# An mLSTM layer with a feed-forward block on one core: the output gates' load and sigmoid moved within the front, gate steps moved to GpSimd, split output weights from the ninth column block on

## The chip, the cores and the metric

The kernel runs on one core of a Trainium2 chip. The time is the device time of one execution in microseconds (us). The kernel before took 531.28 us (median of three runs, 530.12 to 533.42). The clock of TensorE that the chip grants differs between stretches of the run, and the profile shows it beside each.

## The reference

An mLSTM with 4 sequences, 8 heads of width 40 and 768 steps, and behind it a feed-forward block on the 3072 tokens:

```python
m_new = np.maximum(f_gate[:, :, t] + m, i_gate[:, :, t])
f_stab = np.exp(f_gate[:, :, t] + m - m_new)
i_stab = np.exp(i_gate[:, :, t] - m_new)
C = f_stab * C + i_stab * np.einsum('bhd,bhe->bhde', vt, kt)
n = f_stab * n + i_stab * kt
y[:, :, t] = sigmoid(o_gate) * (C @ qt) / np.maximum(np.abs(n . qt), 1.0)
...
h = x @ w_in                                  # x: 3072 x 320, w_in: 320 x 2048
g = np.where(h >= 1, h, np.where(h <= -1, 0.0, (h + 1) ** 2 / 4.0))
out = g @ w_out                               # 2048 x 320
```

The two weights arrive as float64, everything else as float32.

## The kernel before, in words

**Chunks.** The time axis is cut into 6 chunks of 128 steps. An item n = 0 to 23 is one chunk of one sequence (n // 4 is the chunk, n % 4 the sequence). Per item the kernel forms a decay matrix of 128 x 128 for each head (`Abc`: the running sum `ac` of the log decays, written to DRAM as `a_d` and read back broadcast over the partitions, masked by a select on GpSimd, and exponentiated on ScalarE with a bias `nA`), the scores q k (`score`), and in `main` the three parts of the output: `ip`, the carried state times q (`psa<-C,qn`); `up`, values times decayed scores (`psa<-v,Abc`); then on VectorE `hv`, the denominator `z`, `sz`, `y`; then the transpose `psa<-ident,y` and the copies `xh`, `xl` of the result in two words, which the feed-forward block multiplies. `carry_on` makes the new state (`psa<-v,vk`, then `C`). All these products go through the two PSUM buffers `psa`, in turn.

**Gates.** Per chunk, `gate_sums`, `gate_tail` and `gate_exps` (lines 186 to 246) work on 32 x 128 tiles: a scan for m, a clamp and rounding to a grid (`ah`), a scan for `ac`, the rest `a` (stored in `fi_t`) and its scan `al` (stored in `ah`), and the exponents `ex`, which TensorE transposes and ScalarE exponentiates into `G`, the scales of k, v and of the outputs. `dc` is the chunk's total decay; ScalarE makes `dx`, its exponential, which goes through DRAM into `dec`, the factor of the state. In the kernel before all steps but three copies run on VectorE, two of the copies on ScalarE for chunks 1 to 5.

**The feed-forward block.** It runs in six stages j = 0 to 5 of 512 tokens (four items each: stage j multiplies the outputs of items 4j to 4j+3), each with 16 column blocks fc of 128 hidden units. `mm1` (lines 660 to 672) makes eight 128x512 products into one of two `psh` buffers; ScalarE makes relu and its square, VectorE the last step of `r`, which frees the buffer. `mm2` follows two blocks later into four `pso` accumulators. Products are made in two fast words: x is `xh` + `xl`, w_in `wh` + `wl`, w_out `oh` + `ol` and r `gh` + `gl` (`parts`, lines 674 to 679), which gives three passes `oh,gh`, `ol,gh` (named `ow` in the profile) and `oh,gl`. For the first PLAIN_FC blocks of stage 0, r and w_out are multiplied as plain float32 instead, without `gh`, `gl` and without the split of w_out, which is done in stage 1 (lines 801 to 804).

**The weights.** Each of the 16 pieces (8 of w_in for two blocks each, 8 of w_out) is loaded raw (`wraw`, two buffers, two pieces ahead) and turned into float32 words by `words`: `mg` on ScalarE, sign bits (`win<-wraw`, `ow<-wraw`) on VectorE, low bits on GpSimd, then two steps on VectorE; `split` then makes the two fast words, a copy on ScalarE and a subtraction on VectorE. `split_next` (lines 704 to 712) issues one piece; the loop at line 794 calls it until DUE(fc) pieces have been issued. The order of use is in0, in1, out0, in2, out1 and so on.

**What sets the order.** The front (everything before stage 0) is a list of steps by hand, `STEPS`, issued in exactly that order on each engine: L.. are loads, E, A, x the decays of chunk 0, s and m the scores, g and k the gates, o the sigmoid of chunk 0, c and e and d a piece of weights, u, y, z, t the four parts of `main`. Behind it the loop at lines 790 to 821 emits the feed-forward block, and `slot` puts the steps of the items of later chunks between its blocks by the table OFFS. The framework's scheduler then fixes each engine's order by its own estimate of times; `behind` and `issue_after` hold an instruction back behind a named one of the same engine.

Of the kernel before, what the change touches and what calls it, by code (L numbers as in the profile page):

```python
# [13 lines left out]
ALU = mybir.AluOpType  # L14
# [5 lines left out]
L = 128  # L20
# [10 lines left out]
CLAMP = -128.0  # L31

LAG = 2

PLAIN_FC = 16

# [9 lines left out]
ST = 0  # L46

GFC = 3
DUE = lambda fc: 3 + fc

STEPS = (
# [3 lines left out]
)  # L58

HALF = 64  # L60
# [3 lines left out]
GRID = 49152.0  # L64
# [31 lines left out]
def mlstm_ffn_kernel(ctx, tc, qk, qn, vk, og, fi0, fi, w_in, w_out, cst, out):  # L96
# [82 lines left out]
    gtail = {}  # L179

    def gate_piece(c):
        gate_sums(c)
        gate_tail(c)
        gate_exps(c)

    def gate_sums(c):
        pool, i, f = gsrc.pop(c)

        NP = NSEQ if c else 3 * NSEQ
        new = lambda name, p=NP, n=L, bufs=1: pool.tile([p, n], F32, name=name if c else name + "0", bufs=bufs)  # L190
        k = 1
        m, a, ah, ac = new("m", n=L + 1, bufs=k), f, new("ah", bufs=k), new("ac")
        al = ah

        ex = exs[c] = new("ex", P)
        if c:
            nc.vector.tensor_copy(m[:, 0:1], carry)
        else:
            nc.vector.memset(m[:, 0:1], -1e30)
        nc.vector.tensor_tensor_scan(out=m[:, 1:], data0=f, data1=i, initial=m[:, 0:1], op0=ALU.add, op1=ALU.max)  # L200
        nc.vector.tensor_tensor(out=a, in0=f, in1=m[:, :L], op=ALU.add)
        nc.vector.tensor_tensor(out=a, in0=a, in1=m[:, 1:], op=ALU.subtract)

        nc.vector.tensor_scalar(out=ah, in0=a, scalar1=CLAMP, scalar2=GRID, op0=ALU.max, op1=ALU.add)
        nc.vector.tensor_scalar(out=ah, in0=ah, scalar1=-GRID, scalar2=None, op0=ALU.add)
        nc.vector.tensor_tensor_scan(out=ac, data0=rst[:NP], data1=ah, initial=0.0, op0=ALU.mult, op1=ALU.add)
        if c > 0:
            nc.sync.dma_start(a_d[c], ac)
            nc.scalar.copy(ex[64:96], ac)
        else:  # L210

            for p in (2 * NSEQ, NSEQ):
                nc.vector.tensor_tensor(out=ac[:p], in0=ac[:p], in1=top(ac[:p]), op=ALU.subtract)
            T["ac"] = ac
            m, a, ah, ac, al, i = (x[2 * NSEQ:] for x in (m, a, ah, ac, al, i))
            nc.gpsimd.tensor_copy(ex[64:96], ac)
        nc.vector.scalar_tensor_tensor(out=a, in0=a, scalar=CLAMP, in1=ah, op0=ALU.max, op1=ALU.subtract)
        reset = rst[:NSEQ] if c else rst[2 * NSEQ:]
        nc.vector.tensor_tensor_scan(out=al, data0=reset, data1=a, initial=0.0, op0=ALU.mult, op1=ALU.add)
        if c:  # L220
            nc.scalar.mul(ex[96:128], al, -1.0)
        else:
            nc.gpsimd.tensor_scalar(out=ex[96:128], in0=al, scalar1=-1.0, scalar2=None, op0=ALU.mult)
        nc.vector.tensor_copy(carry, m[:, L:])
        gtail[c] = i, m, a, ac, al, ex

    def gate_tail(c):
        i, m, a, ac, al, ex = gtail.pop(c)
        dh = m[:, :L]
        eng = nc.vector  # L230
        eng.tensor_tensor(out=a, in0=i, in1=m[:, 1:], op=ALU.subtract)
        eng.tensor_tensor(out=a, in0=a, in1=al, op=ALU.subtract)
        nc.gpsimd.tensor_copy(ex[0:32], a)
        eng.tensor_tensor(out=dh, in0=ac[:, L - 1:].broadcast_to([NSEQ, L]), in1=ac, op=ALU.subtract)
        eng.tensor_tensor(out=dh, in0=dh, in1=a, op=ALU.add)
        eng.tensor_tensor(out=ex[32:64], in0=dh, in1=al[:, L - 1:].broadcast_to([NSEQ, L]), op=ALU.add)
        eng.tensor_tensor(out=dc[:, c:c + 1], in0=ac[:, L - 1:], in1=al[:, L - 1:], op=ALU.add)
# [466 lines left out]
    def split_next(m="x"):  # L704
        nonlocal nw
        if nw < len(W_ORDER):
            with behind((m, "act"), (m, "dve")):
                for _ in convert(*W_ORDER[nw]):
                    pass
            if nw + 2 < len(W_ORDER):  # L710
                load_w(*W_ORDER[nw + 2])
            nw += 1
# [5 lines left out]
    for what in STEPS.split():  # L718
# [20 lines left out]
        elif what[0] == "m":  # L739
            score_mul(n, hh)  # L740
        elif what[0] == "g":
            gate_sums(n)
        elif what[0] == "k":
            gate_tail(n)
        elif what[0] == "h":
# [44 lines left out]
    for x in range(NG + LAG):  # L790
        j, fc = divmod(x, NFC)
        if x < NG:
            if j == 0:
                while nw < min(len(W_ORDER), DUE(fc)):
                    split_next()
                if nw == len(W_ORDER) and late is None:
                    stages.close()
                    late = ctx.enter_context(tc.tile_pool(name="late", bufs=1, side="right"))
# [9 lines left out]
                    gate_piece(j + 2)  # L808
            r = mm1(j, fc)
            if x == 0:  # L810
                with tc.issue_after(mark["r", "dve"].ins):
                    gate_tail(1)
                    gate_exps(1)
            with behind(("v", "pool")):
                slot(FRONT + x)
            gs[x] = parts(r) if j or fc >= PLAIN_FC else (r,)
# [61 lines left out]
```

## Time and profile before

| What | us |
|---|---|
| median of three runs | 531.28 |
| lowest and highest run | 530.12, 533.42 |
| the profiled execution | 535.73 |
| its span, first to last instruction | 533.9 |
| first matmul of stage 0, of stage 1 | 35.62, 151.07 |
| TensorE (PE) busy in the span | 497.4 |
| VectorE (DVE), ScalarE (ACT), GpSimd (POOL) busy | 366.4, 290.8, 146.4 |
| mean granted clock of TensorE | 0.968 |

A row of a timeline gives start, duration, engine, line, operation and out<-in by the kernel's names; in brackets the idle time before it and what ended it. Most instructions bear line 79, the line of the helper that issues them, or line 82, its branch for the hand-made order of the front; so a row is known by its names. A row of groups gives busy us, the mean of one in ns, and the idle time before.

### The profile page before, as it was taken

How to read it: one execution, taken by the hardware profiler on the slowest of the kernel's cores; microseconds unless marked ns; L12 is line 12 of the kernel's file. 1: busy time of each engine (PE TensorE's matmuls, PEld its weight loads, DVE VectorE, ACT ScalarE, POOL GpSimd, SP SyncE). 2: the span in 40 equal slices, each digit the busy share in tenths (PEclk: the TensorE clock that was granted, in tenths of full speed). 3: DMA queues.
4: the chain of work that ended last, by engine and by line, in shares of the span. 5: the costliest groups of instructions: out<-in, count | busy, mean ns of one | idle time of the engine just before them, and what ended most of it. 6: DMA issues, size and time to landing. Idle time of an engine off the chain costs nothing.

```text
span 533.9 us, 9184 instructions
## 1 busy us (share of the span) xinstructions
PE 497.4 (93%) x3527; PEld 421.8 (79%) x3527; DVE 366.4 (69%) x677; ACT 290.8 (54%) x576; POOL 146.4 (27%) x148
## 2 busy tenths in 40 slices
PE   7985989989899999989999979799999999999996
PEld 4753766768679889879888958598898898989886
DVE  4589988489759777769576848777757756444342
ACT  4525766544458664567644435754468344445553
POOL 2316522234333134343052515152411212000000
PEclk8987999979899999999999979999999999999999
DMA  7858555264342223252122234022333100010001
GB/s 218 243 162 264 182 150 170 83 207 153 85 154 68 48 61 104 79 155 76 30 78 72 84 103 152 3 83 100 111 106 114 40 0 1 2 49 2 1 1 50
DMA packets 29648, 51.31 MB, mean 96 GB/s; under 512 B 10124, under 2 KB 20004, under 8 KB 29604
## 3 DMA queue, kind: packets, MB, share of 16 engines
q1 hardware_dynamic: 29604, 50.72, 31.4%
q8 instruction: 28, 0.46, 0.3%
q14 instruction: 16, 0.13, 0.1%
HBM read 46.67 MB, written 4.04 MB: 95 GB/s over the span
## 4 chain that ended last, share of the span: by engine, by line
PE 69%; DVE 12%; ACT 8%; DMA 6%; issue 2%; POOL 1%; SPq 1%; ACTq 0%; DVEq 0%; POOLq 0%
PE psh L79 29%; PE pso L79 26%; PE psa L79 12%; ACT Abc L79 3%; DMA Abc<-a_d 2%; ACT r L79 2%; DMA wraw<-in_w_out 2%; PE pso L82 1%; DVE win L79 1%; DMA raw<-in_qk 1%; DVE r L79 1%; PE psa L82 1%; DVE mg L79 1%; POOL Abc L79 1%; DVE ow L79 1%
## 5 line engine op out<-in xcount | busy, mean ns | idle before, releaser
L79 ACT ACTIVATE r<-psh,half 128x512 f32<-128x512 f32 x96 | 65.3, 685 | 102.4 <-PE psh L79 101.1
L79 PE MATMUL psh<-xh,wh 128*128 128x512 f32 x288 | 105.6, 422 | 13.4 <-DVE r L79 12.0
L79 DVE SCALAR_TENSOR_TENSOR r<-psh,r 128x512 f32<-128x512 f32 x96 | 66.0, 687 | 65.2 <-ACT r L79 64.9
L79 PE MATMUL psh<-xh,wl 128*128 128x512 f32 x288 | 100.4, 404 | 0.0
L79 PE MATMUL pso<-oh,gh 128*128 128x320 f32 x320 | 99.4, 313 | 0.6 <-ACT gh L79 0.6
L79 PE MATMUL pso<-ow,gh 128*128 128x320 f32 x320 | 98.6, 310 | 0.0
L79 PE MATMUL pso<-oh,gl 128*128 128x320 f32 x320 | 91.1, 310 | 0.0
L79 DVE TENSOR_TENSOR gl<-r,gh 128x512 fp32r<-128x512 f32 x80 | 61.0, 765 | 28.3 <-ACT gh L79 27.7
L79 ACT CAST gh<-r 128x512 fp32r<-128x512 f32 x80 | 49.5, 618 | 51.2 <-DVE r L79 49.9
L79 PEld LDWEIGHTS psh<-xh,wh 128*128 128x128 f32 x288 | 51.8, 195 | 24.1 <-DVE r L79 14.5
L79 PEld LDWEIGHTS psh<-xh,wl 128*128 128x128 f32 x288 | 55.8, 195 | 13.1 <-DVE m L82 0.4
L79 ACT ACTIVATE Abc<-Abc,nA 128x128 f32<-128x128 f32 x160 | 49.6, 390 | 29.7 <-POOL Abc L79 29.7
L79 PEld LDWEIGHTS pso<-oh,gh 128*128 128x128 f32 x320 | 60.1, 188 | 4.5 <-ACT gh L79 0.8
L79 PE MATMUL psh<-xl,wh 128*128 128x512 f32 x192 | 62.5, 408 | 0.0
L79 PEld LDWEIGHTS pso<-ow,gh 128*128 128x128 f32 x320 | 60.1, 188 | 2.8
L79 ACT ACTIVATE r<-r 128x512 f32<-128x512 f32 x96 | 60.3, 632 | 2.2
L79 PEld LDWEIGHTS pso<-oh,gl 128*128 128x128 f32 x320 | 58.0, 188 | 0.3
L79 POOL TENSOR_TENSOR v<-vk,G 128x328 f32<-128x328 f32 x36 | 31.5, 879 | 53.6 <-issue 29.8
L79 POOL TENSOR_TENSOR m<-m 128x1024 bf16<-128x1024 f32 x16 | 31.2, 1953 | 51.8 <-DVE m L79 40.6
L79 PEld LDWEIGHTS psh<-xl,wh 128*128 128x128 f32 x192 | 37.0, 195 | 8.5
L79 PE MATMUL pso<-ow,r 128*128 128x320 f32 x128 | 39.9, 457 | 0.5 <-DVE ow L79 0.5
L79 POOL TENSOR_TENSOR C<-C,dec 120x369 f32<-120x369 f32 x16 | 13.8, 859 | 91.7 <-PE psa L79 91.7
(187 smaller groups left out, 742.0 us busy)
## 6 DMA issues: line engine op xcount, KB each, us to landing
Abc<-a_d SPq DMA_DIRECT2D x20, 512.0 KB
raw<-in_qk SPq DMA_DIRECT2D x48, 160.0 KB
vk<-in_vk SPq DMA_DIRECT2D x20, 324.0 KB
wraw<-in_w_in SPq DMA_DIRECT2D x8, 768.0 KB
wraw<-in_w_out SPq DMA_DIRECT2D x8, 640.0 KB
sig<-in_og SPq DMA_DIRECT2D x6, 640.0 KB
out<-r SPq DMA_DIRECT2D x24, 160.0 KB
qn<-in_qn SPq DMA_DIRECT2D x20, 180.0 KB
```

What stands on the lines that cost most here:

```text
L79: r = getattr(self.engine, name)(*args, **kwargs)
L82: r = getattr(self.engine, name)(*args, **kwargs)
```

## The change

It has these parts.

1. PLAIN_FC is 8 instead of 16: blocks 8 to 15 of stage 0 use the three fast passes, and the second four pieces of w_out are split in stage 0 rather than in stage 1.
2. DUE is 2 + fc instead of 3 + fc, and a piece is held behind the last step of the newest r rather than behind the newest copies of x.
3. In STEPS the load of chunk 0's output gates stands behind the loads of q and k of items 0 and 1, and its sigmoid behind the scores of item 1 instead of ahead of the first decays. The first three parts of chunk 1's gates (ga, gb, gc: `gate_sums` became a generator) and `gate_tail` (k1) are spread over the front; the step d, the subtraction wl of the first piece, comes earlier.
4. For chunks 1 to 5 all gate steps other than scans go to GpSimd, also the two copies into `ex` that ScalarE made; the step with two operations, clamp and subtract, becomes two instructions.
5. `gate_tail(1)` and `gate_exps(1)` are no longer held behind the r of block 0.

```diff
-PLAIN_FC = 16
+PLAIN_FC = 8
...
-DUE = lambda fc: 3 + fc
+DUE = lambda fc: 2 + fc
...
-    "Lg Li Lo Lq0 Lv0 Lq1 Lw0 Lf Lq2 Lv2 Lq3 Lw1 Lc o w9 E0 g0 p A0 k0 x00 w2 s0 x01 m00 w1 E1 A1 h0 v0 x10 m01 w2 s1 "
+    "Lg Li Lq0 Lv0 Lq1 Lo Lw0 Lf Lq2 Lv2 Lq3 Lw1 Lc w9 E0 g0 p A0 k0 x00 w2 s0 x01 m00 w1 E1 A1 h0 v0 x10 m01 w2 s1 "
...
+        eng = nc.gpsimd if c else nc.vector
+        eng.tensor_tensor(out=a, in0=f, in1=m[:, :L], op=ALU.add)
+        eng.tensor_tensor(out=a, in0=a, in1=m[:, 1:], op=ALU.subtract)
+
+        eng.tensor_scalar(out=ah, in0=a, scalar1=CLAMP, scalar2=GRID, op0=ALU.max, op1=ALU.add)
+        eng.tensor_scalar(out=ah, in0=ah, scalar1=-GRID, scalar2=None, op0=ALU.add)
+        if c:
+            nc.vector.tensor_copy(carry, m[:, L:])
+        yield
...
-            nc.scalar.copy(ex[64:96], ac)
+            eng.tensor_copy(ex[64:96], ac)
+            eng.tensor_scalar(out=a, in0=a, scalar1=CLAMP, scalar2=None, op0=ALU.max)
+            eng.tensor_tensor(out=a, in0=a, in1=ah, op=ALU.subtract)
+            yield
...
-        if c:
-            nc.scalar.mul(ex[96:128], al, -1.0)
-        else:
-            nc.gpsimd.tensor_scalar(out=ex[96:128], in0=al, scalar1=-1.0, scalar2=None, op0=ALU.mult)
+        nc.gpsimd.tensor_scalar(out=ex[96:128], in0=al, scalar1=-1.0, scalar2=None, op0=ALU.mult)
...
     def gate_tail(c):
-        eng = nc.vector
+        eng = nc.gpsimd if c else nc.vector
...
-                    split_next()
+                    split_next("r" if fc else "x")
...
-                with tc.issue_after(mark["r", "dve"].ins):
-                    gate_tail(1)
-                    gate_exps(1)
+                gate_exps(1)
```

How the instructions move is shown at three places. The first is ScalarE at the start of stage 0; before, its rows are these (mg and wh belong to a piece of weights, r to the first two blocks, ex and dx to chunk 1's gates):

```order
L79 ACTIVATE mg<-wraw 128x768
L79 CAST wh<-win 128x3x256
L79 ACTIVATE mg<-wraw 128x640
L79 ACTIVATE r<-psh,half 128x512 x2
L79 ACTIVATE r<-r 128x512
L82 COPY ex<-ac 32x128
L79 ACTIVATE r<-r 128x512
L82 ACTIVATE ex<-ah 32x128
L79 ACTIVATE mg<-wraw 128x768
L79 ACTIVATE dx<-dc 32x40
```

In the changed kernel the same place of ScalarE reads:

```order
L79 ACTIVATE mg<-wraw 128x768
L79 ACTIVATE dx<-dc 32x40
L79 CAST wh<-win 128x3x256
L79 ACTIVATE r<-psh,half 128x512
L79 ACTIVATE r<-r 128x512
L79 ACTIVATE mg<-wraw 128x640
L79 ACTIVATE r<-psh,half 128x512
L79 ACTIVATE G<-psa 128x128
L79 ACTIVATE nA<-psa 128x32
L79 ACTIVATE r<-r 128x512
L79 ACTIVATE Abc<-Abc,nA 128x128 x16
L79 ACTIVATE mg<-wraw 128x768
```

The exponential dx of chunk 1's total decay moved from behind the first two blocks' r to ahead of the cast wh and of the first r, the two copies into ex are gone, and sixteen exponentials now stand ahead of the third piece's mg.

The second place is GpSimd in the same stretch of the changed kernel. Its rows ow and win are the low bits of a piece of weights, the selects mask the Abc of chunk 1, and the rows of 32 partitions are the gate steps:

```order
L79 TENSOR_SCALAR ow<-wraw 128x640
L79 AFFINE_SELECT Abc<-Abc 128x1024
L79 TENSOR_SCALAR win<-wraw 128x768
L82 TENSOR_SCALAR ex<-ah 32x128
L82 TENSOR_TENSOR fi_t<-fi_t,m 32x128
L79 AFFINE_SELECT Abc<-Abc 128x1024 x2
L82 TENSOR_TENSOR fi_t<-fi_t,ah 32x128
L82 COPY ex<-fi_t 32x128
L82 TENSOR_TENSOR m<-ac 32x128
L82 TENSOR_TENSOR m<-m,fi_t 32x128
L82 TENSOR_TENSOR ex<-m,ah 32x128
L82 TENSOR_TENSOR dc<-ac,ah 32x1
```

Before, GpSimd had one gate step there (the copy ex<-fi_t), and the three selects came behind it; now the three selects and a piece's step stand ahead of the last six gate steps, the last of which makes dc.

The third place is TensorE at the end of stage 0. Before, the last first products of stage 0 (psh) are followed by these rows, where ow,r is the second product, raw the scores, ident,y the transpose of a main's output, and C,qn, v,Abc and v,vk its other products:

```order
L79 MATMUL pso<-ow,r 128x320 x8
L79 MATMUL psa<-ident,y 128x128 x3
L79 MATMUL psa<-C,qn 128x123 x2
L79 MATMUL psa<-C,qn 128x82
L79 MATMUL psa<-v_1019,Abc 128x41 x8
L79 MATMUL psa<-v_1110,vk 120x123 x3
L79 MATMUL psa<-raw 128x128
L79 MATMUL pso<-ow,r 128x320 x8
L79 MATMUL psa<-raw 128x128 x7
L79 MATMUL psa<-ident,y 128x128 x3
L79 MATMUL psa<-C,qn 128x123 x2
L79 MATMUL psa<-C,qn 128x82
```

In the changed kernel the part of TensorE's order behind the last second products of stage 0, up to the first product of stage 1, is:

```order
L79 MATMUL psa<-ident,y 128x128 x3
L79 MATMUL psa<-C,qn 128x123 x2
L79 MATMUL psa<-C,qn 128x82
L79 MATMUL psa<-v_881,Abc 128x41 x8
L79 MATMUL psa<-v_983,vk 120x123 x3
L79 MATMUL psa<-ident,y 128x128 x3
L79 MATMUL psa<-C,qn 128x123 x2
L79 MATMUL psa<-C,qn 128x82
L79 MATMUL psa<-v_1012,Abc 128x41 x8
L79 MATMUL psa<-v_1114,vk 120x123 x3
L79 MATMUL psa<-raw 128x128 x8
L79 MATMUL psa<-ident,y 128x128 x3
```

Before, two transposes of mains (of items 6 and 7) stood behind the last first products of stage 0; now all four (items 4 to 7) do, three of them in these rows, with no product of the feed-forward block between them.

More of the change, by code (lines that the diff above doesn't have):

```diff
@@ L181, in gate_piece @@
     def gate_piece(c):
-        gate_sums(c)
+        for _ in gate_sums(c):
+            pass
         gate_tail(c)
@@ L200, in gate_sums @@
         nc.vector.tensor_tensor_scan(out=m[:, 1:], data0=f, data1=i, initial=m[:, 0:1], op0=ALU.add, op1=ALU.max)
[L201 to L205, printed above, removed]
+        eng = nc.gpsimd if c else nc.vector
[6 more added lines that the diff above has]
+        yield
         nc.vector.tensor_tensor_scan(out=ac, data0=rst[:NP], data1=ah, initial=0.0, op0=ALU.mult, op1=ALU.add)
@@ L216, in gate_sums @@
             nc.gpsimd.tensor_copy(ex[64:96], ac)
-        nc.vector.scalar_tensor_tensor(out=a, in0=a, scalar=CLAMP, in1=ah, op0=ALU.max, op1=ALU.subtract)
+            nc.vector.scalar_tensor_tensor(out=a, in0=a, scalar=CLAMP, in1=ah, op0=ALU.max, op1=ALU.subtract)
         reset = rst[:NSEQ] if c else rst[2 * NSEQ:]
         nc.vector.tensor_tensor_scan(out=al, data0=reset, data1=a, initial=0.0, op0=ALU.mult, op1=ALU.add)
-        if c:
-            nc.scalar.mul(ex[96:128], al, -1.0)
-        else:
-            nc.gpsimd.tensor_scalar(out=ex[96:128], in0=al, scalar1=-1.0, scalar2=None, op0=ALU.mult)
-        nc.vector.tensor_copy(carry, m[:, L:])
+        nc.gpsimd.tensor_scalar(out=ex[96:128], in0=al, scalar1=-1.0, scalar2=None, op0=ALU.mult)
+        if not c:
+            nc.vector.tensor_copy(carry, m[:, L:])
         gtail[c] = i, m, a, ac, al, ex
@@ L741, in mlstm_ffn_kernel @@
         elif what[0] == "g":
-            gate_sums(n)
+            if hh == 0 and what[1:] not in "bc":
+                sums = gate_sums(n if n == 0 and what == "g0" else 1)
+            next(sums, None)
+            if what == "g0":
+                next(sums, None)
         elif what[0] == "k":
```

4 rows, old and new, of the table STEPS are left out of this document.

## The prediction

> **What bounds the kernel now.** I read the page's first section, then the busy time by stretch, then the waits inside the stretch that the change touches. The page's row of engines:
>
> ```profile
> PE 497.4 (93%) x3527; PEld 421.8 (79%) x3527; DVE 366.4 (69%) x677; ACT 290.8 (54%) x576; POOL 146.4 (27%) x148
> ```
>
> TensorE (PE) is busy 93% of the 533.9 us span, so over the whole program it is the bound, and an engine beside it is worth something only where PE waits. The stretches tell where that is. Columns: length, then busy time (count) of PE, PEld, DVE, ACT and POOL, then clock, DMA share and GB/s. First the front's end to the start of stage 1 and stage 1 itself; then stage 0 cut in two at the r of fc 8 (fc: the column block of 128 hidden units) and its end:
>
> ```profile
> 35.50:151.00 115.50, 100.73 (x491) 77.20 (x492) 92.99 (x162) 62.06 (x129) 44.15 (x42) 0.91 0.53 167
> 151.00:230.00 79.00, 77.22 (x634) 67.98 (x633) 62.77 (x117) 48.74 (x97) 27.19 (x25) 1.00 0.27 81
> ```
> ```profile
> 35.50:87.30 51.80, 43.03 (x186) 31.79 (x186) 47.51 (x82) 33.04 (x69) 22.90 (x20) 0.90 0.65 203
> 87.30:136.50 49.20, 45.63 (x241) 36.46 (x241) 34.43 (x62) 24.47 (x50) 16.16 (x17) 0.93 0.44 140
> ```
>
> From 151 on PE idles 1.8 us of 79. Stage 0 is where time can be had: PE idles 14.8 us of 115.5. In its first half VectorE (DVE) is busy 47.5 of 51.8 us, because every piece of weights is turned from float64 bits into two words there; in the second half DVE has 14.8 us to spare and PE 3.6. So the first half is limited by DVE, the second by PE. The longest single stall, and what surrounds it, in the timeline:
>
> ```profile
> 44.07 0.33 SPq L82 DMA_DIRECT2D a_d<-ac  x1
> ...
> 45.41 1.59 DVE L79 SCALAR_TENSOR_TENSOR ow<-mg,ow 128x640 int32<-128x640 int32 x1
> ...
> 46.47 1.31 POOL L79 TENSOR_SCALAR ow<-wraw 128x640 uint16<-128x640 uint16 x1
> 46.56 1.28 SPq L79 DMA_DIRECT2D Abc<-a_d  x3
> ...
> 47.78 1.22 PE L79 MATMUL psh<-xh,wh 128*128 128x512 f32 x2 [6.41 <-DVE r L79]
> ```
>
> The third group of first-GEMM matmuls waits 6.41 us for DVE's r of fc 0, which stands on DVE behind chunk 1's gate steps and a piece's conversion.
>
> **The change, part by part.** I walk four checkpoints: the third first-GEMM (47.78 before), r of fc 8 (87.3), r of fc 15 (ends 137.2), and the first matmul of stage 1 (151.07).
>
> *Front and start of stage 0.* Sigmoid moves from the head of the front into it. The table switch that this costs again, and the group of the exponentials:
>
> ```profile
> L79 ACT ACT_TABLE_LOAD x3 | 3.8, 1283 | 0.8 <-PEq L867 0.7
> L79 ACT ACTIVATE Abc<-Abc,nA 128x128 f32<-128x128 f32 x56 | 17.3, 390 | 13.7 <-POOL Abc L79 13.7
> ```
>
> The two loads are 2.6 us on ScalarE (ACT), but the output gates' 640 KB no longer stand ahead of the first q and k, and I let the two cancel up to +0.6 us, because DVE also gets chunk 1's scans and a wl subtraction inside the front. If nothing cancels it is +2.6; if the load's lead counts fully, about -2.
>
> Chunk 1's sums now start in the front, so ac is written to a_d some 17 us earlier. What that write meets on the queue is a piece of w_out, here from its issue to the first instruction that uses it:
>
> ```profile
> 24.60 0.35 SPq L82 DMA_DIRECT2D wraw<-in_w_out  x1
> ```
> ```profile
> 32.73 0.91 POOL L79 TENSOR_SCALAR ow<-wraw 128x640 uint16<-128x640 uint16 x1 [12.47 <-DMA wraw<-in_w_out]
> ```
>
> That is 8.1 us. So ac lands between 27.7 (nothing in the way) and about 34 (behind that piece); I take the latter, as the queue is full there. The broadcast Abc lands 4.6 us after its issue (46.56 to the select at 51.17, below), which puts the first select of chunk 1 near 39. The order shows what is new: on GpSimd (POOL) one select, a win step and two selects stand ahead of the last six gate steps, and the dc that these make is awaited by dx on ACT, which stands in front of the wh cast and of the r of fc 0. The rows for the lone small steps and a select:
>
> ```profile
> L82 POOL TENSOR_SCALAR ex<-ah 32x128 f32<-32x128 f32 x1 | 0.5, 529 | 1.0 <-DVE ah L82 1.0
> ```
> ```profile
> 51.17 2.62 POOL L79 TENSOR_SCALAR_AFFINE_SELECT Abc<-Abc 128x1024 f32<-128x1024 f32 x2 [0.92 <-DMA Abc<-a_d]
> ```
>
> 39.1 + select 1.3 + win 1.3 + two small steps 0.8 + two selects 2.6 + six steps at 0.4 (2.4) is 47.5 with dx; then the cast 0.8, relu and square 1.3, and DVE's r 0.7: the third first-GEMM at 50.3, **+2.6 us** against 47.78. If a_d lands at 27.7, POOL is never late and it starts when DVE has done, at about 47.5 or a little before; if the small steps cost 0.7 each, near 53.
>
> *The rest of the first half.* Chunk 1's and 2's gate steps leave DVE: 21 instructions, of which the first and the last group are
>
> ```profile
> L79 DVE TENSOR_TENSOR fi_t<-fi_t,m 32x128 f32<-32x128 f32 x4 | 1.7, 436 | 0.0
> ...
> L79 DVE TENSOR_TENSOR m<-m,fi_t 32x128 f32<-32x128 f32 x2 | 0.5, 264 | 0.0
> ```
>
> 8.2 us in all; with scans and one wl done in the front it is 10.7. Were DVE the only limit, r of fc 8 would come at 87.3 + 2.6 - 10.7 = 79.2; keeping the whole early loss it is 89.9. I take 88.0, near the upper end. In the new order 16 exponentials (16 x 0.39 = 6 us alone, less when run back to back) stand on ACT ahead of the next piece's mg, and another sigmoid with two table loads ahead of the r of fc 8, so that ACT hands DVE its inputs late: **+0.7 us**.
>
> *Second half of stage 0.* PLAIN_FC 16 to 8 gives fc 8 to 15 three fast passes instead of a slow float32 one. Four slow products of one fc, and a group of twelve fast ones by its first and last row:
>
> ```profile
> 131.60 4.47 PE L79 MATMUL pso<-ow,r 128*128 128x320 f32 x16
> ```
> ```profile
> 333.85 0.31 PE L79 MATMUL pso<-oh,gh 128*128 128x320 f32 x1
> ...
> 335.46 0.30 PE L79 MATMUL pso<-oh,gl 128*128 128x320 f32 x1
> ```
>
> 4.47/2 = 2.2 us against (335.46 - 333.85) x 12/11 = 1.76: PE saves 0.48 us per fc, 3.8 us in eight. DVE pays for it: eight subtractions gl, and four subtractions ow that came in stage 1. DVE's groups of stage 0, and gl from the page:
>
> ```profile
> L79 DVE SCALAR_TENSOR_TENSOR r<-psh,r 128x512 f32<-128x512 f32 x16 | 10.9, 683 | 6.8 <-ACT r L79 6.8
> L79 DVE SCALAR_TENSOR_TENSOR ow<-mg,ow 128x640 int32<-128x640 int32 x8 | 9.3, 1167 | 0.0
> L79 DVE SCALAR_TENSOR_TENSOR win<-mg,win 128x768 int32<-128x768 int32 x7 | 7.0, 1004 | 0.2
> L79 DVE TENSOR_SCALAR mg<-mg 128x768 f32<-128x768 f32 x7 | 6.8, 966 | 0.1
> L79 DVE TENSOR_TENSOR wl<-win,wh 128x768 fp32r<-128x768 f32 x7 | 6.7, 953 | 1.4 <-ACT wh L79 1.3
> L79 DVE TENSOR_TENSOR Abc<-psa,Abc 128x512 f32<-128x512 f32 x10 | 6.5, 681 | 6.6 <-PE psa L79 6.6
> L79 DVE TENSOR_SCALAR win<-wraw 128x768 uint16<-128x768 uint16 x7 | 6.3, 897 | 0.1
> L79 DVE TENSOR_SCALAR ow<-wraw 128x640 uint16<-128x640 uint16 x8 | 4.3, 537 | 2.3 <-DMA wraw<-in_w_out 2.3
> ...
> L79 DVE TENSOR_SCALAR mg<-mg 128x640 f32<-128x640 f32 x8 | 3.8, 475 | 0.0
> ...
> L79 DVE TENSOR_TENSOR ow<-ow,oh 128x640 fp32r<-128x640 f32 x1 | 0.8, 812 | 0.0
> ```
> ```profile
> L79 DVE TENSOR_TENSOR gl<-r,gh 128x512 fp32r<-128x512 f32 x80 | 61.0, 765 | 28.3 <-ACT gh L79 27.7
> ```
>
> By the new order DVE does, from behind r of fc 8 to the r of fc 15: 7 r (4.8), 7 gl (5.4), 6 Abc (4.1), four ow pieces with their splits (4 x 2.99 = 12.0), two win pieces (2 x 3.82 = 7.6), and one main's steps, about 4 by the rows of the next fence's kind: 37.9 us. Before, DVE was busy 34.4 of 49.2 us in that stretch, so the bound passes from PE to DVE, and 2 us go to hand-overs between DVE and ACT: 40 us, and r of fc 15 ends at 88.0 + 0.7 + 40 = 128.7, **8.5 us earlier** than 137.2. The bounds are 126.5 (no idle) and 134 (the same idle share as in the first half, and slower subtractions).
>
> *The end of stage 0.* What was hidden is now bare. The new order puts mains 5, 6 and 7 (the mLSTM outputs that stage 1 multiplies) behind all first-GEMMs of stage 0; before, mains 4, 5 and most of 6 stood between them. PE's rows for the one link that was bare, and DVE's y in it:
>
> ```profile
> 135.90 0.49 PE L79 MATMUL psa<-ident,y 128*128 128x128 f32 x3
> ...
> 149.78 0.55 PE L79 MATMUL psa<-ident,y 128*128 128x128 f32 x3 [0.58 <-DVE Abc L79]
> 150.38 0.90 PE L79 MATMUL psa<-C,qn 120*128 120x123 f32 x6
> 151.07 0.71 PE L79 MATMUL psh<-xh,wh 128*128 128x512 f32 x2
> ```
> ```profile
> 144.84 1.26 DVE L79 TENSOR_TENSOR y<-hv,sz 128x320 f32<-128x320 f32 x1
> ```
>
> From one main's transpose (135.90) to the end of the next main's y (146.10) are 10.2 us, of which DVE gave 3.0 to a w_out piece (537, 812, 475 and 1167 ns above), which is done earlier now: 7.2 us a link. Three links are 21.6, ahead of them main 4's transpose and copies with the last C and gl, 3.4 (an estimate from 535, 765 and two copies), behind them main 8's C product, 0.7: 25.7 us where before 13.9 stood. Stage 1 starts at 128.7 + 25.7 = 154.4, **+3.3 us**. Bounds of this term: links of 6 us give 150.8, of 8.5 us 158.3.
>
> *After 151.* Stage 1 loses four splits of ACT and DVE; its PE idles 1.8 us of 79: **-0.5** (0 to -1.8). In stage 3 a gate piece stands on DVE in front of an r:
>
> ```profile
> 338.04 0.73 PE L79 MATMUL psh<-xh,wh 128*128 128x512 f32 x2 [2.27 <-DVE r L79]
> ```
>
> Off DVE it can give back up to 2.3 us; but the same chain now runs through 14 POOL steps, so **-1.0** (0 to -2.3). At the boundary to stage 4 the order has a main's transpose directly ahead of the first matmul: **+0.5** (0 to +2). Elsewhere PE has no gaps to win or lose.
>
> Sum: +0.6 and +2.6 are spent by r of fc 8 (+0.7); then +3.3 at stage 1; -0.5 - 1.0 + 0.5 gives **+2.3 us**. The profiled execution took 535.73 us with a span of 533.9, and the median of the runs is 531.28, 4.45 lower; I put the difference on the median: **533.6 us**, slower by 0.4%.
>
> **A rule weighed.** At 45.41 DVE's ow step took 1.59 us while POOL's ran from 46.47, against a mean of 1.17. The Trainium skill, SBUF — State Buffer, section SBUF: two separate sides, says that DVE with two SBUF inputs and a GpSimd operation that reads SBUF hold a shared pair of ports exclusively, and the loser waits whole. The trace agrees in direction with 0.4 us of the 0.5 us overlap. By that rule the 20 small steps moved in stage 0 could each stop DVE for their length, 8 us at most, and the sum would be up to +10.
>
> **Rivals.** *POOL keeps up* (faster). If ac lands at 27.7, POOL's steps cost about 0.3 and dx waits for nothing: the third first-GEMM at 47.5, r of fc 8 at 83, r of fc 15 at 123.7, and with links of 6.5 us (23.6 in all) stage 1 at 147.3, -3.8; with -0.5 and -1.5 behind it 525.5. For it: DVE has 10.7 us less to do where it is 92% busy. Against it: the full queue at 24.60 and dx's new place ahead of r.
>
> *POOL becomes the pacemaker* (slower). Its place is the small-step chain, chunk 1's ahead of dx and chunk 2's ahead of the next pieces' win and ow steps. From about 0.6 us a step it decides: at 0.7, six steps make the third first-GEMM 53 or later (+2.7 on my walk), and chunk 2's 14 steps cost 4.2 more before DVE can go on with a piece; +7 reaches the saturated second half, which has no slack to absorb it: 540.6. For it: the lone row of 529 ns and the slowed ow step. Against it: POOL is busy only 44 of 115.5 us in the stage. The rule above works through the same chain.
>
> *Work only moved* (no change). The four splits and eight gl cost in stage 0 what PE saves, the bare tail is as long as the second half's gain, and the order's new lead for the pieces changes nothing since each is still converted right ahead of the r that follows: 531.3. This is also how it would look if the earlier conversion did not do what it says.
>
> **How the numbers follow.** My walk 0.45, with its own range 529 to 539 from the tail's bounds; POOL keeps up 0.25; POOL the pacemaker 0.18; work only moved 0.12. About 1% (5.3 us) is what a measurement of this kernel can tell from no change. Faster by more: 0.03 of my walk, 0.21, 0 and 0.01, together 0.25. Within: 0.28, 0.04, 0.01 and 0.10, together 0.43. Slower: 0.14, 0, 0.17 and 0.01, together 0.32. The range, 523 to 543, takes in both outer rivals with some 2 us to spare.
>
> **What would show it.** The third first-GEMM near 50, with dx ahead of r waiting for POOL; PE's idle in the second half put down to DVE; r of fc 15 ending near 129; three bare links of 7 us before the first matmul of stage 1, near 154; no 2.3 us wait near 338. It is wrong if the third first-GEMM starts before 47.8, if mains 5 to 7 take under 6 us a link, or if PE still waits for DVE's r by several us in fc 4 to 8.

## The result, and the profile after

The changed kernel takes 548.76 us (median of four runs, 547.19 to 552.91), the kernel before 531.38 in the same runs. The ratio is 1.0335 (95% interval 1.027 to 1.0401): 17.4 us slower, where 2.3 were forecast and the range ended at 543. The first row of its page:

```profile
PE 497.6 (91%) x3556; PEld 425.5 (78%) x3559; DVE 357.8 (66%) x630; ACT 293.6 (54%) x575; POOL 180.5 (33%) x218
```

PE's busy time is that of before (497.4), DVE has 8.6 us less, POOL 34 more. So in sum nothing was added to the busiest engine: the time went into its waiting.

The profiled execution of before took 535.73 us, above the four runs here, so the kernel before was profiled a second time, with a span of 529.0. In it the r of fc 0 starts 5.3 us earlier than in the trace that the prediction was read from (47.04 there, in the timeline of stage 0's start):

```profile
41.77 0.69 DVE L79 SCALAR_TENSOR_TENSOR r<-psh,r 128x512 f32<-128x512 f32 x1
```

From there on the two traces run 4.5 to 5.7 us apart. Most of the delay arose in the front: the first matmul of stage 0 stands at 31.27 instead of 35.62. Of these 4.4 us, 1.7 are waits of PE for loads of q and k, which the second trace does not have; where the rest comes from was not traced. All comparisons below use the second trace. By the start of the r steps on DVE:

| stretch | before, second trace | changed | difference |
|---|---|---|---|
| start to r of fc 0 | 41.8 | 45.8 | +4.0 |
| fc 0 to fc 8 of stage 0 | 42.2 | 42.5 | +0.2 |
| fc 8 to fc 15 | 46.8 | 35.9 | -10.9 |
| fc 15 to stage 1's first r | 20.8 | 39.8 | +19.0 |
| stages 1 and 2, to stage 3's first r | 163.5 | 161.7 | -1.8 |
| stage 3, first to last r | 74.4 | 70.3 | -4.1 |
| stage 3's last to stage 4's first r | 9.3 | 16.5 | +7.2 |
| stage 4's first to stage 5's first r | 69.6 | 73.3 | +3.7 |
| stage 5's first r to the end | 60.7 | 59.7 | -1.0 |

They sum to the 16.4 us between the spans (529.0 and 545.4), but for rounding. The second row hides a swing: the r of fc 2 comes 10.1 us later than before, that of fc 7 only 1.1. Two boundaries carry the loss. The columns of the stretches are those of the prediction: length, then busy time (count) of PE, PEld, DVE, ACT and POOL, then clock, DMA share and GB/s. Before, second trace, the end of stage 0 and that of stage 3:

```profile
130.80:151.50 20.70, 17.91 (x135) 13.62 (x133) 13.51 (x25) 7.14 (x17) 8.07 (x8) 0.92 0.39 117
...
389.00:398.70 9.70, 9.47 (x96) 8.36 (x95) 5.72 (x13) 5.68 (x10) 1.48 (x2) 1.00 0.31 93
```

The same in the changed kernel:

```profile
124.10:163.90 39.80, 31.89 (x219) 27.67 (x217) 23.30 (x49) 12.57 (x36) 13.95 (x16) 0.74 0.42 129
...
395.90:412.40 16.50, 13.82 (x129) 11.91 (x128) 10.30 (x20) 8.34 (x17) 5.12 (x5) 1.00 0.50 154
```

PE idles 7.9 us in the first (2.8 before), and works at a clock of 0.74 there, so that its busy time grows too. Where this begins shows in PE's timeline much earlier. The transpose of chunk 2's exponents, the first scores of item 4 and main 4's first product of values, before (second trace):

```profile
62.32 0.27 PE L79 MATMUL psa<-ident,ex 128*128 128x128 f32 x1
...
65.36 0.82 PE L79 MATMUL psa<-raw 40*128 40x128 f32 x4 [2.13 <-DVE C L79]
...
88.78 1.47 PE L79 MATMUL psa<-v,Abc 128*128 128x41 f32 x12
```

and in the changed kernel:

```profile
77.95 0.33 PE L79 MATMUL psa<-ident,ex 128*128 128x128 f32 x1 [1.78 <-POOL ex L79]
83.57 0.48 PE L79 MATMUL psa<-raw 40*128 40x128 f32 x2
...
107.27 1.92 PE L79 MATMUL psa<-v,Abc 128*128 128x41 f32 x16
```

The transpose is 15.6 us later, the scores 18.2, the product 18.5. The transpose stands ahead of the scores in PE's order and in the turn of the two psa buffers, in both kernels; scores of item 4 are the first link of a serial chain (mains 4 to 7) that must end before stage 1. So that chain starts 18 us late, and the time that it needs lies bare behind the last first products. Two things make the transpose late. Counted in PE's rows, it stands behind the first products of eight column blocks, before behind those of six. And when PE has come to it, it waits 1.78 us more for the last of the 14 gate steps, now on POOL in between pieces of weights:

```profile
62.25 2.05 POOL L79 TENSOR_TENSOR fi_t<-fi_t,m 32x128 f32<-32x128 f32 x2
64.39 0.92 POOL L79 TENSOR_SCALAR ow<-wraw 128x640 uint16<-128x640 uint16 x1
...
68.27 1.77 POOL L79 COPY ex<-ac 32x128 f32<-32x128 f32 x1
...
77.51 0.39 POOL L79 TENSOR_TENSOR ex<-m,ah 32x128 f32<-32x128 f32 x1
```

From the first step to the last are 15.7 us. Single gate steps in these rows take from 0.39 to 1.77 us, and two more steps of pieces stand in the rows left out. Which of the two counts, the place in the order or the engine, is what the runs with all gates on DVE decide below.

### The profile page after: what moved, and what is told of

Same layout as the page of the kernel before. It is cut to its first block, busy times and chain, and to the rows that moved or that the text cites. A ratio compares the mean times of both kernels' runs of the same rounds, so it can differ in the third digit from the quotient of the medians.

```text
span 545.4 us, 9279 instructions
## 1 busy us (share of the span) xinstructions
PE 497.6 (91%) x3556; PEld 425.5 (78%) x3559; DVE 357.8 (66%) x630; ACT 293.6 (54%) x575; POOL 180.5 (33%) x218
## 4 chain that ended last, share of the span: by engine, by line
PE 60%; DVE 14%; ACT 8%; issue 3%; DMA 3%; POOL 3%; ACTq 0%; DVEq 0%; POOLq 0%; SPq 0%
PE psh L79 26%; PE pso L79 22%; PE psa L79 12%; ACT Abc L79 3%; ACT r L79 3%; DVE r L79 2%; DVE gl L79 2%; DVE ow L79 1%; DVE C L79 1%; DVE win L79 1%; DVE z L79 1%; DVE hv L79 1%; ACT L79 1%; DVE m L79 1%; DVE mg L79 1%
## 5 line engine op out<-in xcount | busy, mean ns | idle before, releaser
L79 PE MATMUL pso<-ow,gh 128*128 128x320 f32 x352 | 108.8, 311 | 0.8 <-DVE ow L79 0.8
L79 PE MATMUL pso<-oh,gh 128*128 128x320 f32 x352 | 107.7, 312 | 0.2 <-ACT oh L79 0.2
L79 PE MATMUL psh<-xh,wl 128*128 128x512 f32 x288 | 103.1, 409 | 0.5 <-DVE wl L79 0.5
L79 PE MATMUL pso<-oh,gl 128*128 128x320 f32 x352 | 103.2, 313 | 0.0
L79 DVE TENSOR_TENSOR gl<-r,gh 128x512 fp32r<-128x512 f32 x88 | 66.9, 762 | 28.6 <-ACT gh L79 27.8
L79 ACT CAST gh<-r 128x512 fp32r<-128x512 f32 x88 | 54.5, 619 | 56.1 <-DVE r L79 54.9
L79 PEld LDWEIGHTS pso<-ow,gh 128*128 128x128 f32 x352 | 66.2, 188 | 4.7 <-DVE ow L79 1.3
L79 PEld LDWEIGHTS pso<-oh,gh 128*128 128x128 f32 x352 | 65.9, 188 | 3.9 <-ACT oh L79 0.7
L79 PEld LDWEIGHTS pso<-oh,gl 128*128 128x128 f32 x352 | 64.4, 188 | 1.3
L79 PE MATMUL psa<-raw 40*128 40x128 f32 x320 | 33.6, 298 | 1.4 <-DVE hv L79 1.4
```

Source lines behind the costliest of these rows:

```text
L79: r = getattr(self.engine, name)(*args, **kwargs)
```

## The experiments

Each ran against the kernel before on the same chip; ratios are to it, with a 95% interval. The changed kernel stands at 1.0335.

**The kernel before once more.** Unchanged.

> The kernel before, unchanged, for a second trace. All theories: 530 to 534 us. It tells how much of the 4.4 us by which the first profiled execution (535.73) stood over the median is in the kernel's stages and how much in the run: if the span is near 530, the differences between the two first traces have to be read some 4 us larger, and the stretch where they lie shows in the times of the r steps.

Ratio 0.9996 (0.9953 to 1.0039), span 529.0. The surplus of the first trace was in the run, and most of it in its front, as shown above.

**Pieces held behind x instead of r** (changed kernel):

```diff
-                    split_next("r" if fc else "x")
+                    split_next()
```

> The changed kernel with one word undone: a weight piece is held behind the newest copies of x again, not behind the newest r; everything else as changed. Theory 'bare boundaries' (the loss is mains that the scheduler put behind the last first products of stage 0 and of stage 3): the order of TensorE shows mains 5 and 6 back among fc 12 to 15, so stage 1's first r comes about 6 us earlier and the time is near 542; stage 3 to 4 stays as it is. Rival 'GpSimd contention' (the moved gate steps slow VectorE all along): no gate step is touched, so 548 to 549. Rival 'clock' (the slower runs have a lower granted clock, 0.954 to 0.962 against 0.968, whatever the order): within 2 us of 548.8.

558.12 us, 1.0489 (1.0435 to 1.0542): slower by 9 us instead of faster by 6. Every theory missed. Mains 5 and 6 did go back between the first products, but the first products then stood behind them: r of fc 12 came at 129.3 where the changed kernel has 109.3, stage 1's first r at 170.5 against 164.0. Only part of that is waiting: from 100 to 132 PE idles 4.2 us, and its granted clock is 0.50 from 104 to 124. In these two kernels, whose chains start at 102.0 and 106.6, putting the chain between the first products instead of behind them does not help.

**Chunk 5's gate steps alone on DVE** (changed kernel):

```diff
-eng = nc.gpsimd if c else nc.vector
+eng = nc.gpsimd if 0 < c < 5 else nc.vector
```

> The changed kernel with the gate steps of chunk 5 alone back on VectorE (chunks 1 to 4 stay on GpSimd). Theory 'bare boundaries': TensorE's order at the boundaries of stage 3 to 4 and 4 to 5 is again that of the kernel before, worth 6.8 and 2.2 us in the traces, less some 2 us that stage 3 gains from having these steps off VectorE: near 542; stage 0 keeps its bare tail. Rival 'GpSimd contention': 14 of 68 steps are taken away, a fifth of the loss: 545. Rival 'clock': within 2 us of 548.8.

540.52 us, 1.0165 (1.0111 to 1.022): 8 us back, 1.5 more than the theory of the boundaries had. The trace shows what the boundary hangs on: again a transpose. Chunk 5's sums are stored (a_d) and its exponents transposed, before (second trace):

```profile
331.09 0.32 SPq L79 DMA_DIRECT2D a_d<-ac  x1
```
```profile
334.93 0.41 PE L79 MATMUL psa<-ident,ex 128*128 128x128 f32 x1
```

in the changed kernel:

```profile
344.12 0.32 SPq L79 DMA_DIRECT2D a_d<-ac  x1
```
```profile
354.98 0.27 PE L79 MATMUL psa<-ident,ex 128*128 128x128 f32 x1
355.09 0.49 PE L79 MATMUL psa<-ident,y 128*128 128x128 f32 x3
```

and with chunk 5 on DVE:

```profile
341.93 0.32 SPq L79 DMA_DIRECT2D a_d<-ac  x1
```
```profile
345.04 0.30 PE L79 MATMUL psa<-ident,ex 128*128 128x128 f32 x1 [0.61 <-DVE ex L79]
```

From the store to the transpose it is 3.8, 10.9 and 3.1 us, and a main's own transpose (ident,y) stands right behind in the turn of psa. So mains 16 to 19 start late, and main 19 ends behind the last product of stage 3. There the wait has company: the load of the next output gates is issued at 398.91, when main 19's `sz`, which reads the old ones, is done, and the table load and the sigmoid stand ahead of the xh cast for which stage 4 waits. Changed kernel, ACT and then PE:

```profile
403.28 1.28 ACT L79 ACT_TABLE_LOAD   x1 [0.44 <-DMA sig<-in_og]
404.58 1.27 ACT L79 ACTIVATE sig<-sig 128x1280 f32<-128x1280 f32 x1
405.75 0.46 ACT L79 CAST xh<-psa 128x384 fp32r<-128x384 f32 x1
```
```profile
406.27 0.72 PE L79 MATMUL psh<-xh,wh 128*128 128x512 f32 x2 [1.58 <-ACT xh L79]
```

**Both edits** (pieces behind x, chunk 5 on DVE).

> The changed kernel with both: pieces held behind the copies of x, and chunk 5's gate steps on VectorE. Theory 'bare boundaries': both losses go, 534 to 536, within 1% of the kernel before. Rival 'GpSimd contention': chunks 1 to 4 still on GpSimd, 545. Rival 'clock': 547.

547.23 us, 1.0295 (1.0234 to 1.0355). The theory (534 to 536) is missed. The number that "clock" gave, 547, fits, but that rival had held the two single edits to be without effect, and they moved the time by 9 us up and 8 down. The second edit is again worth some 10 us (from 1.0489), the first again costs.

**Chunk 2's transpose later.** From here on the theory is that of the late scores. Changed kernel with only the place of `gate_exps(2)` moved, that is of the transpose and of the two steps on ACT that read it (G and nA); the gate steps stay on POOL:

```diff
         gate_tail(c)
-        gate_exps(c)
+        if c != 2:
+            gate_exps(c)
...
-            if x == 0:
-                gate_exps(1)
+            if x in (0, 8):
+                gate_exps(2 if x else 1)
```

> The changed kernel with one step moved: the transpose of chunk 2's exponents and its exponentials (gate_exps of chunk 2) are issued at fc 8 instead of with the other gate steps at fc 3; the gate steps stay on GpSimd. In the changed kernel that transpose stands in TensorE's order and in the turn of the psa buffers ahead of the scores of item 4, and ran at 77.95, where the second trace of before has it at 62.3; main 4's product of values follows at 107.3 against 88.8. Theory 'late scores' (that queue place delays the serial chain of mains 4 to 8, which then lies bare at the end of stage 0): scores of item 4 go to about 55, main 4's product near 80, stage 1's first r 8 to 12 us earlier, time 537 to 541. Rival 'GpSimd contention': no step leaves GpSimd, 548 to 549. Rival 'bare end by the hold behind r': the hold is unchanged, 548.

538.15 us, 1.0113 (1.004 to 1.0186): within the number. PE's rows in the order expected:

```profile
60.52 1.79 PE L79 MATMUL psa<-raw 40*128 40x128 f32 x16
...
80.02 1.92 PE L79 MATMUL psa<-v,Abc 128*128 128x41 f32 x16
...
95.09 0.27 PE L79 MATMUL psa<-ident,ex 128*128 128x128 f32 x1
```

Scores 23 us earlier than in the changed kernel, main 4's product 27 us earlier, stage 1's first r at 156.9 instead of 164.0, 7.1 us where 8 to 12 were expected. The transpose at 95 holds nothing up: the next rows of PE wait for r.

**Both places mended**: chunk 2's transpose at fc 8, chunk 5 on DVE.

> The run before this one with chunk 5's gate steps on VectorE in addition, which alone took 8.3 us off the changed kernel (540.5). Theory 'late scores': both gains add up, 529 to 533. Rivals: 540 to 541, what chunk 5 alone gives.

528.96 us, 0.9945 (0.991 to 0.9981): the gains add up, and this kernel is a little faster than the one before.

**All gate steps on DVE** (changed kernel, `eng = nc.vector`; two of them, the negation and a copy into ex, are on POOL in any case).

> The changed kernel with all gate steps back on VectorE, the rest as changed. In its order of TensorE chunk 2's transpose still stands ahead of item 4's scores at fc 8, and the boundary of stages 3 and 4 is that of before. Theory 'late scores': stage 0 hardly gains by the engine, the time is that of chunk 5 alone on VectorE, 539 to 542. Rival 'GpSimd contention': the whole loss goes, 531 to 534.

536.82 us, 1.0087 (1.005 to 1.0125): 13 us back, between the two expectations. The exponents are done at 71.8, but the transpose still stands behind the first products of eight column blocks and comes without a wait at 75.6, and the scores wait for nA on ACT, which reads the transpose. DVE, then PE:

```profile
71.48 0.28 DVE L79 TENSOR_TENSOR ex<-m,ah 32x128 f32<-32x128 f32 x1
```
```profile
75.62 0.27 PE L79 MATMUL psa<-ident,ex 128*128 128x128 f32 x1
...
79.59 0.53 PE L79 MATMUL psa<-raw 40*128 40x128 f32 x2 [1.16 <-ACT nA L79]
```

So 13.3 of the transpose's 15.6 us of lateness are there without the engine. Stage 1's first r is at 158.5: some 5 us of stage 0 are the engine, 3.7 of them at the r of fc 0 (42.1, before 41.8), and 7 stay.

**Gate steps on POOL in the kernel before** (part 4 alone).

> The kernel before with the change's part 4 alone: gate steps other than scans of chunks 1 to 5 on GpSimd. In the order chunk 2's transpose moves by about one fc, and the boundaries of stages 3 to 4 and 4 to 5 get the order of the changed kernel. Theory 'late scores' with the boundary: 8 us from the boundaries and up to 3 in stage 0, 538 to 542. Rival 'GpSimd contention': about the whole loss, 545 or more.

552.77 us, 1.0389 (1.0312 to 1.0466): 21 us slower, no less than the whole change. The theory's size was missed, and the rival's number fits; but the trace has the loss at the two transposes. Here PE waits 6.2 us for the engine at chunk 2's. Chunk 2's, with its wait:

```profile
74.06 0.47 PE L79 MATMUL psa<-ident,ex 128*128 128x128 f32 x1 [6.17 <-POOL ex L79]
76.40 2.08 PE L79 MATMUL psa<-raw 40*128 40x128 f32 x16 [0.64 <-DVE C L79]
```

11.7 us behind the second trace of before, stage 1's first r 11.5 behind; chunk 5's is 12.3 us after its store, and the stretch from stage 3's last r to stage 4's first is 7.1 us longer.

**A fourth buffer for Abc** (changed kernel, `bufs=4`).

> The changed kernel with a fourth buffer for Abc (the decay matrices of an item), nothing else; TensorE's order in stage 0 is the same as in the changed kernel. There each of the three bare links at the end of stage 0 runs from one Abc load to the next (129.2, 137.4, 147.6, then stage 1 at 155.9): main's product frees the buffer, 3.4 us of load, select, 2.4 us of exponentials, and only behind them on ScalarE the xh cast that frees psa. Theory 'links paced by the Abc reload': with one buffer more the load is done before, links fall from 8 to 10 us to about 6, stage 1's first r comes 5 to 8 us earlier, 541 to 544. Rival 'links paced by VectorE's steps from hv to y', as the prediction had it: 548 to 549.

546.28 us, 1.0297 (1.0206 to 1.0387). That is no difference from the changed kernel that the interval would show, and stage 1's first r comes at 167.8, no earlier. The loads still start when the product of the same main ends, so the links were not freed as meant, and the test is no clean one. But its rows speak against the theory of the Abc reload. ACT and PE in one link:

```profile
146.33 0.48 ACT L79 CAST xh<-psa 128x384 fp32r<-128x384 f32 x1 [5.46 <-PE psa L79]
146.86 2.45 ACT L79 ACTIVATE Abc<-Abc,nA 128x128 f32<-128x128 f32 x8
```
```profile
139.70 1.95 PE L79 MATMUL psa<-v,Abc 128*128 128x41 f32 x16 [0.68 <-DVE hv L79]
141.88 0.86 PE L79 MATMUL psa<-v,vk 128*120 128x123 f32 x6 [0.23 <-DVE xh L79]
145.42 0.87 PE L79 MATMUL psa<-ident,y 128*128 128x128 f32 x3 [2.67 <-DVE y L79]
146.08 1.41 PE L79 MATMUL psa<-C,qn 120*128 120x123 f32 x6
147.71 3.60 PE L79 MATMUL psa<-v,Abc 128*128 128x41 f32 x16 [0.22 <-DVE xh L79]
```

Here the xh cast comes ahead of the exponentials, and waited for PE's transpose, which waited for DVE's y; the link is still 8.0 us. That is the prediction's link (7.2), plus a slow clock (0.50 from 144 on in this trace).

**PLAIN_FC 8 alone** (kernel before).

> The kernel before with part 1 alone (PLAIN_FC 8). TensorE's order keeps the scores and mains where before has them. By the walk of the prediction TensorE saves 0.48 us in each of eight fc and the splits leave stage 1; VectorE has the room in the second half (34 of 49 us busy), so the saving shows: 527 to 530. Rival 'the second half becomes bound by VectorE': 532 to 536.

535.01 us, 1.0064 (1.0024 to 1.0105): it costs, and the rival's number fits. From r of fc 8 to that of fc 15 it takes longer (r of fc 15 at 138.9 against 130.8), of which 5 us are won back by stage 1's first r.

**PLAIN_FC 8 and chunk 2's transpose at fc 8** (kernel before).

> The kernel before with PLAIN_FC 8 and chunk 2's transpose and exponentials issued at fc 8; gate steps on VectorE as before. Theory 'late scores': scores of item 4 come before 62, main 4's product some 5 us earlier, and with part 1's saving 522 to 528. If the scores' place costs the kernel before nothing, the same as part 1 alone.

532.06 us, 0.9988 (0.9951 to 1.0026): no difference to the kernel before, and the number was missed. Next to the run before this one the later transpose is worth 0.8%, with intervals that just touch.

**The mended kernel with a fourth buffer for Abc.**

> The run with chunk 2's transpose at fc 8 and chunk 5's gate steps on VectorE (528.96), with the fourth buffer for Abc in addition. Theory 'links paced by the Abc reload': the last link or two at the end of stage 0 shorten, 523 to 527. Rival: 528 to 530.

543.62 us, 1.0197 (1.0111 to 1.0283): by the ratios 13 us slower than without, where both theories had it no slower. The buffer changed the scheduler's order in several places; which of them costs this was not settled.

**Chunk 2's gate steps alone on DVE** (changed kernel).

> The changed kernel with chunk 2's gate steps alone on VectorE (chunks 1, 3, 4, 5 stay on GpSimd); its transpose keeps its place ahead of item 4's scores in TensorE's order. If the engine makes the transpose late (a chain of 14 short steps behind selects and pieces in GpSimd's queue), the scores start some 5 us earlier and the time is 543 to 545, the part of the stage 0 loss that all gates on VectorE took back. If only the queue place counts, 548 to 549.

548.04 us, 1.0286 (1.0217 to 1.0354): the median is that of "only the queue place counts", but the interval also reaches a gain of 5 us. The trace says the same as that of all gates on DVE: the last exponent is done at 75.0, and the transpose moved only from 78.0 to 76.7, the scores from 83.6 to 82.7.

**The mended kernel with all gates on DVE.**

> The kernel with chunk 2's transpose at fc 8 and all gate steps on VectorE (no part 4 at all). If GpSimd's gate steps are of use once they hold up nothing, this is slower than the 528.96 of the kernel with chunks 1 to 4 on GpSimd by 2 to 5 us, as 8 us of VectorE come back into stage 0. If the engine only costs, it is 525 to 528.

530.73 us, 0.9981 (0.995 to 1.0013). Against 0.9945 the intervals overlap: the steps of chunks 1 to 4 on POOL gain some 0.4%, which is not told apart from nothing, and show no cost once no queue waits for them. Against all gates on DVE with the transpose in its old place only `gate_exps(2)` differs, and stage 1's first r comes at 151.0 instead of 158.5, where before has it at 151.6. So the 7 us that the engine left in stage 0 are the place of this transpose. The six runs of the changed kernel's order together, as ratios:

| gate steps on POOL | transpose of chunk 2 in its place | at fc 8 |
|---|---|---|
| chunks 1 to 5 | 1.0335 | 1.0113 |
| chunks 1 to 4 | 1.0165 | 0.9945 |
| none | 1.0087 | 0.9981 |

**The mended kernel with PLAIN_FC 16.**

> The kernel with chunk 2's transpose at fc 8 and chunk 5's gates on VectorE, with PLAIN_FC back at 16. Part 1 alone cost the kernel before 0.6%. If the fast passes cost more on VectorE than they save on TensorE, 524 to 527; if they pay once the mains start early, 531 to 534.

535.3 us, 1.0056 (1.0025 to 1.0086), clear of 0.9945 and of its interval: here the fast passes pay, 1.1%. The stretch 84 to 134 (first PE, PEld, then DVE) tells why. With PLAIN_FC 16:

```profile
84.00:134.00 50.00, 48.32 (x243) 36.82 (x242) 38.73 (x62) 27.65 (x52) 17.19 (x16) 1.00 0.43 140
```

and with 8:

```profile
84.00:134.00 50.00, 42.95 (x268) 36.91 (x267) 47.09 (x79) 32.15 (x63) 17.54 (x16) 1.00 0.43 141
```

PE is relieved of 5.4 us, DVE takes 8.4 more and is then 94% busy: with 16 PE is the bound of this stretch, with 8 it is DVE. That this pays here and not in the kernel before goes with main 4, whose product is there at 76.3 and in the kernel before at 88.8; a run that separates the two was not made.

**The mended kernel with part 2 undone.**

> The kernel with chunk 2's transpose at fc 8 and chunk 5's gates on VectorE, with part 2 undone (pieces as early as before, held behind the copies of x). Its order of TensorE has mains 4 to 7 spread over fc 8 to 15 as in the kernel before. If the bare end of stage 0 by the hold behind r costs anything, 523 to 527; if the serial chain of mains takes its time wherever it stands, 528 to 531 or more.

531.93 us, 0.9973 (0.9935 to 1.0012): not told apart from 0.9945. In the mended kernel the hold behind r is neither a loss nor a gain that shows.

## Why the prediction was wrong, point by point

The prediction's own steps, each as the change in its length, with the measured change between the second trace of before and the changed kernel:

| step | forecast | measured |
|---|---|---|
| start to the r that it called that of fc 8 | +0.7 | +1.1 |
| from it to the end of the r of fc 15 | -9.2 | -7.7 |
| end of that r to the first matmul of stage 1 | +11.8 | +17.1 |
| from there to the end | -1.0 | +5.9 |
| sum | +2.3 | +16.4 |

The sum is that of the two spans; the medians are 17.4 apart. Two steps failed: the end of stage 0, too short by 5.3 us, and what comes after 151, off by 6.9. (The r at 87.3 in the first trace is that of fc 7; fc 8's starts at 89.44. The table keeps to the same r in all traces.)

- **Front and start of stage 0** (+2.6): right in mechanism. dx on ACT waited 9.25 us for POOL's dc and r stood behind it; the third first-GEMM came at 46.55. Against the second trace's 42.52 that is +4.0. The walk's own number for it, 50.3, was 3.7 too late, as POOL's six steps were done at 43.5 rather than 47.5. So its sign of being wrong, a start before 47.8, came true by the base and not by the mechanism.
- **The rest of the first half** (+0.7, "Chunk 1's and 2's gate steps leave DVE"): the number held at its r, but here the mechanism was missed that makes the end bare. The prediction counted the steps that leave DVE and asked what POOL delays on ACT. It did not follow chunk 2's chain to its end, the transpose, behind which the scores of item 4 stand in the turn of psa. The scores were 18 us late without this showing at the r of fc 7 (+1.1) or fc 8 (+4.3). With all gates on DVE they are still 14 late, so most of that is the order and not POOL. Moving that one transpose took back 10.6 us.
- **Second half** (r of fc 15 at 128.7): the saturated DVE was right (busy 33.6 of 35.9 us from fc 8 on), and the length nearly: 41.9 us from the same r, where 40.7 were forecast. That PLAIN_FC pays was not tested in the changed kernel itself; taking it back costs the mended kernel 1.1%, and putting it alone into the kernel before costs 0.6%.
- **The end of stage 0** (25.7 us): the bare mains were read from the order, without asking what put them there, and the three bare links were right in kind and too short. They are 8.1, 8.5 and about 12 us by the products at 127.3, 135.4, 143.9 and the first product of stage 1, and part of that is the clock, 0.50 from 140 on. The end took 31.0 us, from 124.9 to 155.9. PE's rows in it:

```profile
135.38 1.95 PE L79 MATMUL psa<-v,Abc 128*128 128x41 f32 x16 [0.68 <-DVE hv L79]
...
143.87 3.60 PE L79 MATMUL psa<-v,Abc 128*128 128x41 f32 x16 [0.68 <-DVE hv L79]
...
155.86 1.22 PE L79 MATMUL psh<-xh,wh 128*128 128x512 f32 x2 [1.45 <-ACT xh L79]
```

- **The base of the sum.** The walk gave 154.4 for the start of stage 1, and it came at 155.9. That is luck: the trace that it started from is late by its front, so that the walk's 88.0 stands for an r that came at 83.0, and the two steps behind it were 6.5 us too short. Against the second trace, where that matmul stands at 145.41, stage 1 starts 10.4 us later, not 3.3.
- **"At the boundary to stage 4 ... +0.5 (0 to +2)"** and **"Elsewhere PE has no gaps to win or lose"**: the second failure. The order was read, but the bare main was not priced as a chain, nor chunk 5's transpose behind the POOL steps. It is +7.2 at stage 4 and +3.7 up to stage 5; putting chunk 5's steps back on DVE takes 8.2 us off, so here the cause is the engine. The gain inside stage 3 (-1.0) is there and larger, -4.1.
- **The rivals.** POOL the pacemaker (540.6) named a right engine, with the price at the wrong place: it looked for the delay at r of fc 0 and at the pieces of weights, and found 7 us; the queue behind the transposes makes it 21 in the kernel before, and the order of the change adds its own part. The Trainium skill's rule of the shared ports (SBUF — State Buffer, section SBUF: two separate sides), named beside it, is not what the loss hangs on: with chunk 2's transpose later and chunk 5 on DVE, the same steps of chunks 1 to 4 on POOL cost nothing that can be measured (0.9945 with them, 0.9981 without). Nor does the row given for it agree: that section gives the ports to whichever operation starts first, and the slowed DVE step had begun 1.1 us before POOL's.

What stays open: which of the parts 2, 3 and 5 moves chunk 2's transpose behind two more column blocks (PLAIN_FC alone leaves it behind six), and why the fourth buffer costs 13 us in the mended kernel.

## What to carry to other kernels

When a chain of small steps moves, to another engine or in the order, follow its result to the first in-order queue or rotating buffer in which something else stands behind it, and price the lateness of that, not the busy time that was moved. A step that nothing needs soon (here the transpose of a later chunk) belongs behind the steps that start a serial chain. Test the place and the engine apart, since either can make the same step late. And take the base of a sum from two executions.

## What the runs showed of the hardware

The granted clock fell at the bare end of stage 0 and stayed down. Stretches of 4 us of the changed kernel (PE busy first, the clock behind POOL's column):

```profile
140.00:144.00 4.00, 2.21 (x10) 2.05 (x10) 1.42 (x3) 1.62 (x6) 1.82 (x2) 0.50 0.28 90
144.00:148.00 4.00, 4.00 (x19) 4.00 (x20) 1.20 (x3) 1.19 (x4) 0.46 (x2) 0.50 0.17 46
...
156.00:160.00 4.00, 4.00 (x10) 3.13 (x11) 1.45 (x4) 0.00 (x0) 0.78 (x2) 0.50 0.35 99
160.00:164.00 4.00, 3.52 (x58) 2.76 (x56) 0.44 (x2) 2.65 (x6) 0.34 (x1) 0.99 0.04 16
```
```profile
143.87 3.60 PE L79 MATMUL psa<-v,Abc 128*128 128x41 f32 x16 [0.68 <-DVE hv L79]
147.27 1.56 PE L79 MATMUL psa<-v,vk 128*120 128x123 f32 x6
148.77 2.78 PE L79 MATMUL psa<-raw 40*128 40x128 f32 x16
```

It was 1.00 up to 136 and 0.50 from 140 to 160, though PE's longest single wait there is the 2.7 us ahead of 141.1. In the second trace of before it fell to 0.57 in one such stretch only, from 136 to 140. The Trainium skill (TensorE: Matmul & The Clock Gate, Part 1: The HAM clock gate) has half speed after an idle window of about 3.4 us, and full speed after a busy one of the same length. The two speeds agree with these rows. The rest does not show in them: no gap was 3.4 us long, and by the records the small products from 143.9 to 151.5 follow each other without a gap, for 7.7 us, and did not bring the clock back; the 512-column products from 155.9 on did by 160. The same sixteen products took 1.95 us at 135.4 and 3.60 at 143.9, and the first pair of first products of stage 1 took 5.7 us (155.9 to 161.6) against 3.8 in the kernel before. So a bare serial chain is paid twice, as idle time and in the clock. On POOL a copy of 32 x 128 took 1.77 us at 68.3 and 0.28 at 75.0, so a chain of 14 such steps cannot be priced by one row.
